# A recurrence and an MLP on one core: weight pieces dealt anew over the first four units, two turnings placed apart, and a little MLP work kept back

## The chip, the cores and the metric

The kernel runs on one core of one Trainium2 chip. The metric is device time in microseconds of one execution; the time of a kernel is the median of its runs. One further execution is profiled, and all views of the profile are of that one.

## What is computed

A gated linear recurrence over 768 steps for 4 batches and 8 heads of width 48, then an MLP over all 3072 tokens:

```python
f = 1.0 / (1.0 + np.exp(-f_logit))
for t in range(S):
    state = f[:, :, t, :, None] * state + np.einsum('bhd,bhe->bhde', k[:, :, t], v[:, :, t])
    y[:, :, t] = np.einsum('bhd,bhde->bhe', q[:, :, t], state)
x = y.transpose(0, 2, 1, 3).reshape(B * S, H * D)     # 3072 x 384
h = x @ w_in                                          # 384 x 2048
out = (h * (1.0 / (1.0 + np.exp(-1.702 * h)))) @ w_out
```

The MLP's arrays come as 64-bit floats. Their bits are read as pairs of 32-bit words, and the core makes 32-bit floats of them.

## The kernel before

**Units.** The tokens are cut into twelve units of 256 tokens (three for each batch). A unit's recurrence is done in chunks of 64: six levels of scores (`score`, L384), masked on VectorE (`evacuate`, L410), added into y (`add`, L448), with q and k multiplied by products of gates after each level (`promote`, L436 and L437, or L439 for both at once). `set_aside` (L423, ScalarE) keeps copies Kc and Qc of what the next level reads. `turn_k` (L505, L506) turns k through TensorE and copies it as kn. The states follow (products L523, chain on VectorE L538 to L543), then y takes what earlier states give (L563), is copied (L571) and brought to the MLP's layout xT by DMA (L592, L597). The first three units use a level at a time (parts "W"); from unit 3 on two levels go together (parts "V").

**Turnings.** Each unit's f, q and k arrive by rows and are turned: `begin_f` makes F = sigmoid(f), `begin` the q part of X, `begin_k` the k part. For units 0 to 2 TensorE turns them (L339, L342), from unit 3 on VectorE does (`nc.vector.transpose`, L327), and ScalarE adds the sigmoid of F (L332). After a turning SP's queue loads the same array for the unit after (`load_raw`), four DMAs each.

**Weights.** The 64-bit weights are 32 pieces, 128 columns of w_in or 128 rows of w_out each, fetched two at a time (`fetch_weights`, L180) into three buffers named bits. ScalarE makes a first copy `a` (L208), and five operations on VectorE make the piece (`chain`, L219 to L228). `convert` emits one such operation. When a pair is done, the next fetch is issued. A step of the MLP names how many pieces have to be done before it.

**MLP steps.** An h step is three matmuls with 256 columns (768 columns, L727), a sigmoid on ScalarE (sg, L732) and a product on VectorE (g, L733). An o step is one matmul of 384 columns (L755); each group of four is added into `sum` (L791, L793). From unit 3 on the second product runs as seven products of half size (L704), which need differences T of w_out, made on VectorE (`sums_of_b`, L622). PSUM's banks for h, o and the turnings are four, tag "mm".

**Order.** TensorE's order is the order of the program throughout. For the other engines it is so up to `fill_order.close()`, after unit 3; behind that a planner orders them. `merge(n, ...)` walks over the parts of unit n, and after each part emits MLP steps ("fill") up to a share of `columns`, and conversions up to a share of `pieces`. The shares come from `steady`: W 3, V 4, S 3, and 1 each for T, B and K. "Marks" below are the boundaries between merges: behind the first one the rest of unit 1 (its y and xT) comes at the head of unit 2, behind the second that of unit 2 at the head of unit 3. `hold=1` in merge 1 leaves its first part without fill. `UNIT` is 24576 columns, `LAG` 6912, `DM` 384.

For unit 2 the parts are W six times, B (f and q of unit 3), T, T, B (k of unit 3), S; for units from 3 on they are V three times, B (f and q), T, T, B (k), S.

Of the kernel before, what the change touches and what calls it, by code (L numbers as in the profile page):

```python
# [23 lines left out]
def kernel(  # L24
# [34 lines left out]
    B, H, S, D = q.shape  # L59
    DM = H * D  # L60
# [170 lines left out]
    def convert():  # L231

        if state["begin"] < len(pairs) and len(todo) <= NOP:
            begin_pair(state["begin"])
            state["begin"] += 1
        if todo and todo[0]:
            todo.pop(0)()
        if todo and todo[0] is None:
            todo.pop(0)
            state["done"] += 2  # L240
            fetch_weights()
# [34 lines left out]
    def load_vl(n, l):  # L276

        if n >= NALL:
            return
        t = vls[n, l] = ld.tile([P, DM], F32, tag=f"vl{l}", name=f"vl_{n}_{l}")  # L280
        if n < N_TURN:
            pt = ps.tile([P, DM], F32, tag="mm", name=f"tv_{n}_{l}", bufs=4)
            for g in range(NG):
                nc.tensor.matmul(
                    pt[g * 64:(g + 1) * 64], lhsT=perm[:, l - 1, :] if l else ident[:, ::2], rhs=vns[n][:, g, :],
                    start=True, stop=True,
                )
            nc.scalar.copy(t, pt)  # L288
            return
        nc.sync.dma_start(out=t, in_=v_toks[n % 2].rearrange("(n two m) e -> two n m e", two=2, m=LEV[l])[0])  # L290
# [507 lines left out]
    def mlp_blocks(*blocks):  # L798

        hs, os = zip(*(mlp_block(n, r) for n, r in blocks))  # L800
        return sum(hs, []) + sum(os, [])


    def keep_up(times):

        if times:
            pt = ps.tile([P, NL * 64], F32, tag="mm", name=f"idle_{next(serial)}", bufs=4)
        for _ in range(times):
            nc.tensor.matmul(pt, lhsT=ident, rhs=masks.rearrange("p l t -> p (l t)"), start=True, stop=True)

    units = [attention(n) for n in range(NALL)]
    LAG = 18 * DM

    def parts_of(n):

        parts = list(units[n][1])
        _, inter = parts.pop()
        if n:
            kind, scores = parts[0]
            _, ahead = units[n - 1][1][-1]  # L820
            parts[0] = kind, lambda: (ahead(), scores())
        if n < N_TURN:

            def with_v(l):
                kind, fn = parts[l]
                return kind, lambda: (fn(), load_vl(n, l) if n == 0 or l else None, keep_up(2 * (n == 0 and l < 3)))
            parts[:NL] = [with_v(l) for l in range(NL)]
        if n + 1 < NALL:
            begin_f, begin, begin_k, begin_gates = units[n + 1][0]
            i = len(parts)  # L830
            if n + 1 < N_FILL:

                parts.append(("K", lambda: (begin_k(), begin_gates(), load_vl(n + 1, 0) if n + 1 < N_TURN else None)))
                parts.insert(i - 4, ("B", begin if n == 0 else lambda: None))
                parts.insert(i - 5, ("B", begin_f))
                if n:

                    kind, head = parts[0]
                    parts[0] = kind, lambda: (head(), begin())
            else:  # L840
                kind, states = parts.pop()
                parts += [("B", begin_k), (kind, lambda: (states(), begin_gates()))]
                parts.insert(i - 3, ("B", lambda: (begin_f(), begin())))
        else:
            parts.append(("W", inter))
        return parts

    def merge(n, fill, columns, share, pieces=0, hold=0, by=1.0, chores=()):

        parts = parts_of(n)
        total = sum(share(kind) for kind, _ in parts)
        converting = {"W": 3, "T": 3, "B": 1} if n < N_FILL - 1 else {"W": 3, "V": 4, "S": 3, "T": 1, "B": 1}
        total_ops = sum(converting.get(kind, 0) for kind, _ in parts)
        held = sum(share(kind) for kind, _ in parts[:hold])
        at = at_ops = done = ops = 0
        for kind, fn in parts:
            ready = state["done"]
            fn()  # L860
            for chore in chores[:2]:
                chore()
            chores = chores[2:]
            at += share(kind)
            at_ops += converting.get(kind, 0)
            n_ops = min(int(pieces * NOP * at_ops / (by * total_ops)), pieces * NOP) - ops
            ops += n_ops
            first, n_columns = done, max(0, columns * (at - held) / (total - held) - done)

            def some(end):  # L870
                nonlocal done
                while fill and done < end and fill[0][2] <= ready:
                    w, emit, _ = fill.pop(0)
                    emit()
                    done += w
            for i in range(n_ops):
                some(first + n_columns * i / n_ops)
                convert()
            some(first + n_columns)
# [4 lines left out]
    UNIT = NFF * NK * U + U // P * NFF * DM  # L884
# [12 lines left out]
        load_raw(1, j)  # L897
    load_vn(1)
    fill = []
    merge(0, fill, 0, steady, 8)  # L900
    fill += mlp_blocks((0, 0)) + mlp_blocks((0, 1))
    merge(1, fill, UNIT // 2 - LAG // 2, steady, 10, hold=1)
    fill += mlp_blocks((1, 0), (1, 1)) + mlp_blocks((0, 2), (1, 2))
    merge(2, fill, UNIT, steady, 8)
    fill += mlp_blocks((2, 0), (2, 1)) + mlp_blocks((2, 2), (0, 3)) + mlp_blocks((1, 3), (2, 3))
    merge(3, fill, 3 * UNIT // 2 - LAG // 2, steady, 6, by=0.7)
    fill_order.close()
    for n in range(3, NALL):
        fill += mlp_unit(n)
# [33 lines left out]
```

## Time and profile before

| | us |
|---|---|
| median of 5 runs | 657.02 (655.54 to 658.23) |
| the profiled execution | 658.5 |
| its span, first to last instruction | 656.5 |
| TensorE busy (matmul; weight load) | 634.0; 543.2 |
| VectorE busy | 444.3 |
| ScalarE, GpSimd busy | 229.2; 60.1 |
| a turning on VectorE (L327) | 2.04 |
| the five operations of a piece | 0.35, 0.55, 0.35, 0.55, 0.54 to 0.59 |
| an h step, an o step on TensorE | 1.30, 0.65 |

The span is what lies between the first and the last instruction; the execution's own time has some 2 us around it. A matmul of 32-bit floats stands in the trace as two records, so an h step is six. The profile names engines PE (matmul), PEld (weight load), DVE (VectorE), ACT (ScalarE), POOL (GpSimd) and SP; a "q" behind the name is that engine's queue. "L327" is a line of the kernel. In lines of waits, "A <- B" says that A waited and B ended the wait.

### The profile page before, as it was taken

The page shows a single profiled execution, that of the slowest core. Times are in us where ns is not written, and L with a number is a line of the kernel's source. Part 1 is how long each engine was busy: PE and PEld are TensorE (multiplying, and loading weights), DVE is VectorE, ACT ScalarE, POOL GpSimd, SP SyncE. Part 2 cuts the span into 40 slices and gives each one's busy share as a digit, 9 for nine tenths or more (in the row PEclk, how much of TensorE's full clock was granted, in tenths as well). Part 3 has the DMA queues.
Part 4 walks back from the last instruction along what each step waited for, and adds up shares of the span by engine and source line. Part 5 has one row for each costly group of instructions (what it writes and reads, how often), then busy time and mean ns, then how long its engine had stood idle before and what let it go on. Part 6 is the DMA issues. An engine that isn't in the chain of part 4 may idle for free.

```text
span 656.5 us, 20397 instructions
## 1 busy us (share of the span) xinstructions
PE 634.0 (97%) x8958; PEld 543.2 (83%) x8958; DVE 444.3 (68%) x802; ACT 229.2 (35%) x477; POOL 60.1 (9%) x116
## 2 busy tenths in 40 slices
PE   6978989999999999999999999999999999999997
PEld 5655767766678689989989989989989989989997
DVE  2987977788887757657658658558558557553571
ACT  3454543243223423323324324324324334222120
POOL 3050020020001002002002002002002002000000
PEclk9998999999999999999999999999999999999999
DMA  8877875294125444524524524614604202101000
GB/s 185 223 198 186 210 180 130 81 225 82 37 64 148 136 105 111 151 50 119 148 44 121 150 43 120 163 29 120 166 27 104 67 25 62 39 2 26 25 1 24
DMA packets 67554, 67.67 MB, mean 103 GB/s; under 512 B 30410, under 2 KB 61290, under 8 KB 67466
## 3 DMA queue, kind: packets, MB, share of 16 engines
q1 hardware_dynamic: 67466, 66.38, 40.5%
q8 instruction: 70, 1.15, 0.8%
q14 instruction: 18, 0.15, 0.1%
HBM read 56.92 MB, written 8.65 MB: 100 GB/s over the span
## 4 chain that ended last, share of the span: by engine, by line
PE 86%; DVE 7%; DMA 3%; ACT 2%; issue 1%; SPq 1%; DVEq 0%; ACTq 0%
PE h L727 37%; PE o_X L704 7%; PE o L755 7%; PE o_Y L704 7%; PE o_Z L704 7%; PE sc L384 5%; PE y L448 5%; PE o_W L704 4%; PE t L339 2%; PE y L563 2%; PE sc L523 1%; DMA bits<-in_moe_w_in_dram 1%; PE tkn L505 1%; DMA xT<-yT 1%; DVE X L439 1%
## 5 line engine op out<-in xcount | busy, mean ns | idle before, releaser
L727 PE MATMUL h<-xT,w_in 128*128 128x256 f32 (+1 forms) x1152 | 261.4, 383 | 6.3 <-DMA xT<-yT 3.9
L727 PEld LDWEIGHTS h<-xT,w_in 128*128 128x128 f32 x1152 | 216.2, 191 | 40.1 <-issue 4.8
L733 DVE TENSOR_TENSOR g<-h,sg 128x256 f32<-128x256 f32 (+1 forms) x192 | 80.7, 422 | 99.9 <-ACT sg L732 97.4
L732 ACT ACTIVATE sg<-h 128x256 f32<-128x256 f32 (+1 forms) x192 | 73.3, 383 | 195.7 <-PE h L727 189.6
L423 ACT COPY Kc<-X 128x512 f32<-128x512 f32 x69 | 46.2, 670 | 118.7 <-DVE X L439 84.7
L755 PE MATMUL o<-w_out,g 128*128 128x384 f32 x192 | 66.1, 493 | 0.0
L439 DVE TENSOR_TENSOR X<-X,tot 128x1024 f32<-128x1024 f32 x45 | 55.1, 1224 | 15.4 <-PE sc L384 10.2
L755 PEld LDWEIGHTS o<-w_out,g 128*128 128x128 f32 x192 | 35.3, 190 | 22.9 <-issue 1.4
L704 PE MATMUL o_X<-w_out,g 128*128 128x192 f32 x288 | 51.9, 329 | 0.0
L704 PE MATMUL o_Y<-T,S 128*128 128x192 f32 x288 | 51.1, 331 | 0.1
L704 PEld LDWEIGHTS o_Y<-T,S 128*128 128x128 f32 x288 | 46.5, 190 | 2.6 <-DVE u L679 1.2
L704 PEld LDWEIGHTS o_X<-w_out,g 128*128 128x128 f32 x288 | 47.3, 190 | 0.9
L410 DVE TENSOR_TENSOR A<-sc,masks 128x512 f32<-128x512 f32 x72 | 46.7, 679 | 0.0
L376 POOL TENSOR_TENSOR tot<-F 128x512 f32<-128x512 f32 x12 | 12.5, 1040 | 342.6 <-DVE st L540 342.6
L448 PE MATMUL y<-A,vl 64*48 64x64 f32 x2304 | 40.9, 217 | 0.4 <-ACT vl L288 0.4
L448 PEld LDWEIGHTS y<-A,vl 64*48 64x48 f32 x2304 | 36.0, 120 | 3.8 <-issue 3.1
L327 DVE STREAM_TRANSPOSE X<-raw 128x1024 f32<-128x1024 f32 x18 | 36.7, 2039 | 2.5 <-PE y L563 2.5
L571 ACT COPY yT<-y 48x512 f32<-48x512 f32 x48 | 27.8, 580 | 14.0 <-PE y L563 13.5
L384 PEld LDWEIGHTS sc<-X,Kc 48*64 48x64 f32 x1344 | 23.9, 134 | 8.6 <-issue 3.8
L384 PE MATMUL sc<-X,Kc 48*64 48x64 f32 x1344 | 28.2, 220 | 1.8 <-DVE A L410 1.1
L376 POOL TENSOR_TENSOR tot<-tot 128x256 f32<-128x256 f32 (+4 forms) x60 | 27.3, 455 | 4.7
L357 POOL COPY q_last<-X 128x4 f32<-128x4 f32 x12 | 14.1, 1178 | 144.1 <-DVE X L327 111.8
(93 smaller groups left out, 675.4 us busy)
## 6 DMA issues: line engine op xcount, KB each, us to landing
vl<-v_tok SPq DMA_DIRECT2D x60, 192.0 KB, 2.9
bits<-in_moe_w_out_dram SPq DMA_DIRECT2D x8, 768.0 KB, 9.1
bits<-in_moe_w_in_dram SPq DMA_DIRECT2D x8, 576.0 KB, 9.0
v_tok<-in_v_dram SPq DMA_DIRECT2D x10, 384.0 KB, 4.4
vn<-v_tok SPq DMA_DIRECT2D x10, 384.0 KB, 7.1
xT<-yT SPq DMA_DIRECT2D x24, 144.0 KB, 2.8
raw<-in_q_dram SPq DMA_DIRECT2D x18, 192.0 KB, 4.0
raw<-in_f_logit_dram SPq DMA_DIRECT2D x18, 192.0 KB, 4.8
```

Of the source, the lines that this page charges most:

```text
L327: nc.vector.transpose(out.rearrange("p (a i j) -> p a j i", a=NP, j=R), raw[:, j].rearrange("p a (j d) -> p (a j) d", j=R)[:, :, :32],)
L376: nc.gpsimd.tensor_tensor(tn, t2[:, :, 0], t2[:, :, 1], ALU.mult)
L384: nc.tensor.matmul(out[g * HS:(g + 1) * HS, h, a, :], lhsT=lhs(h, a * U + g * G), rhs=rhs(h, a * U + g * G), start=True, stop=True,)
L410: nc.vector.tensor_tensor(A[:, :, c:c + w].rearrange("p h (x t) -> p h x t", t=64), t["sc"][:, :, c:c + w].rearrange("p h (x t) -> p h x t ...
L423: nc.scalar.copy(c.rearrange("p (n m) -> p n m", m=m), X[:, j, :NA].rearrange("p (n two m) -> p n two m", two=2, m=m)[:, :, hf, :],)
L439: nc.vector.tensor_tensor(qk, qk, by, ALU.mult)
L448: nc.tensor.matmul(dst(h, g, a), lhsT=vls[n, u][g * 64:(g + 1) * 64, (2 * a + h) * D:(2 * a + h + 1) * D], rhs=A(h, g, a), start=(start an ...
L704: nc.tensor.matmul(t[bank], lhsT=lhs(f), rhs=rhs(f), start=(new and f == 0), stop=(f == HF - 1), skip_group_check=True,)
L727: nc.tensor.matmul(ph, lhsT=w_in[:, c, ff * P:(ff + 1) * P], rhs=xTs[n][:, c, :], start=(c == 0), stop=(c == NK - 1))
L732: nc.scalar.activation(sg, ph, AF.Sigmoid, scale=1.702)
L733: nc.vector.tensor_tensor(g[ff // FG][:, ff % FG, :], ph, sg, ALU.mult)
L755: nc.tensor.matmul(t["po"], lhsT=g[ff // FG][:, ff % FG, tt * P:(tt + 1) * P], rhs=w_out[:, ff, :], start=(ff == ffs[0]), stop=(ff == ffs[ ...
```

## The change

Three edits. The first places the turning of q one part later than that of f, between the two T parts, for units from 3 on; this adds a part of share 1 to each of these units (25 shares become 26 in unit 2, 19 become 20 in later ones). The second deals the 32 pieces over the first four units as 6, 10, 9, 7 where it was 8, 10, 8, 6. The third takes 1152 columns of fill (3 x 384) out of merge 1 and puts them into merge 3; merge 2 has as many as before, so the kept steps pass through it.

```diff
             else:
                 kind, states = parts.pop()
                 parts += [("B", begin_k), (kind, lambda: (states(), begin_gates()))]
-                parts.insert(i - 3, ("B", lambda: (begin_f(), begin())))
+                parts.insert(i - 3, ("B", begin_f))
+                parts.insert(i - 1, ("B", begin))
...
-    merge(0, fill, 0, steady, 8)
+    merge(0, fill, 0, steady, 6)
     fill += mlp_blocks((0, 0)) + mlp_blocks((0, 1))
-    merge(1, fill, UNIT // 2 - LAG // 2, steady, 10, hold=1)
+    merge(1, fill, UNIT // 2 - LAG // 2 - 3 * DM, steady, 10, hold=1)
     fill += mlp_blocks((1, 0), (1, 1)) + mlp_blocks((0, 2), (1, 2))
-    merge(2, fill, UNIT, steady, 8)
+    merge(2, fill, UNIT, steady, 9)
     fill += mlp_blocks((2, 0), (2, 1)) + mlp_blocks((2, 2), (0, 3)) + mlp_blocks((1, 3), (2, 3))
-    merge(3, fill, 3 * UNIT // 2 - LAG // 2, steady, 6, by=0.7)
+    merge(3, fill, 3 * UNIT // 2 - LAG // 2 + 3 * DM, steady, 7, by=0.7)
     fill_order.close()
```

## The prediction, made before the changed kernel was run

> **What bounds the kernel now.** First I read the share of the span on the page (TensorE 97%), then cut the span into stages with the table of busy times by stretch. Its columns are the stretch, its length, then busy us and count for PE, PEld, DVE, ACT and POOL, then granted clock, DMA share and GB/s.
>
> ```profile
> 20.00:42.00 22.00, 18.35 (x478) 13.66 (x478) 22.00 (x50) 11.63 (x24) 5.08 (x1) 1.00 0.85 204
> 42.00:56.00 14.00, 9.66 (x216) 7.14 (x213) 8.89 (x21) 7.93 (x15) 5.07 (x10) 0.95 0.62 155
> 56.00:86.00 30.00, 30.00 (x505) 20.94 (x506) 28.43 (x68) 13.70 (x30) 0.00 (x0) 0.97 0.89 230
> 86.00:126.00 40.00, 38.30 (x533) 28.20 (x533) 29.71 (x64) 13.79 (x29) 3.63 (x6) 1.00 0.53 128
> 126.00:158.00 32.00, 28.38 (x318) 20.08 (x317) 27.61 (x47) 12.45 (x26) 3.75 (x8) 1.00 0.71 155
> 206.00:600.00 394.00, 393.92 (x5885) 356.73 (x5884) 256.49 (x414) 139.32 (x292) 35.55 (x62) 1.00 0.35 90
> ```
>
> From 206 to 600 us TensorE is idle for 0.08 us: nothing can be won there, only lost. All idle time that the change can reach lies before 158 us. Unit 0 (to 42 us) is VectorE's: 22.00 of 22. Unit 1 (56 to 86) is full on both, TensorE 30.00 and VectorE 28.43. After that TensorE bounds, with short gaps. Second view, TensorE's waits between 92 and 160 us (total, times, longest):
>
> ```profile
> PE h L727 <- DMA xT<-yT: 1.9, 2, 1.7
> PE h L727 <- ACT kn L506: 1.3, 1, 1.3
> PE y L563 <- DVE st L543: 0.7, 2, 0.5
> PE h L727 <- DVE sum L793: 0.5, 1, 0.5
> PE h L727 <- DVE g L733: 0.5, 1, 0.5
> ```
>
> The first is unit 1's first h step waiting for its xT; 1.7 of it lies at 95.8 us, behind the first mark. The second is at 131.8 us, and the timeline shows why: VectorE turns f and q back to back, F's sigmoid waits for the first, and the copy kn that frees a PSUM bank stands behind it on ScalarE.
>
> ```profile
> 127.79 2.04 DVE L327 STREAM_TRANSPOSE F<-raw 128x1024 f32<-128x1024 f32 x1
> 129.68 2.01 DVE L327 STREAM_TRANSPOSE X<-raw 128x1024 f32<-128x1024 f32 x1
> 34.51 0.99 ACT L208 ACTIVATE a<-bits 128x384 f32<-128x384 f32 x2 [2.04 <-DMA bits<-in_moe_w_out_dram]
> ```
>
> The last line is needed below: in unit 0 ScalarE stood 2.04 us for the fourth pair of weight pieces, which lands at 34.5 us.
>
> **What the Trainium skill says.** "Perfetto Trace Analysis", section Identifying the Most-Contended Engine, warns that TensorE's matmul share is no measure of how near it is to its peak, and offers the weight-load share. The trace agrees in direction: 97% matmul, 83% weight load. I therefore count idle time and not the share. The same page, section Optimizing Scalar/DVE Operations, says that an unsaturated VectorE that still causes bubbles elsewhere may be helped by breaking its work up; at 126 to 158 us it is 27.61 of 32 busy and makes the 1.3 us bubble, so that is the case of the split. "TensorE: Matmul & The Clock Gate", section What's actually happening, says that an idle window of about 3.4 us halves the clock. The trace has clock 0.95 and 0.97 in the second and third stretch, around the idle time before unit 0's first h steps: 12 records took 4.47 us there, against 2.59 later in the chain. That 1.9 us may come, go or move, and I put it into the range alone.
>
> **The deal of pieces, unit 0.** A piece costs VectorE five operations: from the groups of 14 to 42 us 0.351, 0.558, 0.345, 0.543 and 0.543 us, sum 2.34. Two pieces less are 4.68, and since neighbours overlap by about 0.08 each (start to start is shorter than the duration), ten operations are 4.68 - 0.8 = 3.9 us. One pair of ScalarE's a copies (1.0) goes too, and one fetch of 768 KB from SP's queue before unit 0 ends. VectorE is never idle there, so the 3.9 us lie on the path up to the state chain at 42.2 us. What is late next: the fourth pair's bits still land at 34.5, because SP issues them right behind unit 1's loads. Their a copies (1.0 us) now hold back the copies kn; from VectorE's side the last eleven operations end near 38.3, from ScalarE's side the second kn ends near 36.7, then 1.0 us of products. So the chain starts near 38.4, 3.8 earlier; I take **-3.6**, with 0 and -3.9 as the ends.
>
> **Unit 1.** It has ten pieces in both, at the same places, one pair later in the list. Its fill is taken until 8832 columns are reached, which whole steps make 9216 (eight h, eight o); with 7680 it is six h and eight o. So 1536 columns move, two h steps of 1.30 us (six records in the chain), 2.6 us of TensorE. VectorE sets the end: the third state product ends at about 86 us, just when TensorE arrives at y. Only one g (0.42) leaves the queue ahead of it, the other stood behind. So TensorE falls idle for 2.6 - 0.4 = 2.2 us at y: the removed fill shows as a gap. Behind the mark it comes back. Before, from y at 85.95 to h at 95.81 is 9.86 us, 1.9 of it waiting, thus about 7.9 of work. After, work is 7.9 + 2.6 = 10.5, longer than the path of xT (four copies, SP's issues, a landing), so the wait is gone. Net: -0.4 + (10.5 - 9.9) = **+0.2**; ends -1 and +1. By itself the shift of columns wins nothing here.
>
> **Unit 2.** Nine pieces for eight: five operations, 2.2 us, and two g more. From 86 to 126 us VectorE has 10.3 us free, so most of it is hidden beside fill. The end is not hidden: from F at 127.79 to the third state product at 143.2 VectorE is the chain (two turnings, four g, eight conversions, k's turning, 1.29 us for ScalarE's Kc and Qc, promote 1.23). After, F starts earlier: at 18/26 of the fill for 18/25, 681 columns or 1.15 us. F and q are apart, so F's sigmoid and kn follow while one turning (2.0) fits in the four PSUM banks (4 x 1.30 us), and the 1.3 us stall goes. But the chain has six g for four (+0.84). TensorE, free at T, waits at y for what VectorE still lacks. Net -1.15 + 0.84 = **-0.3**; ends +2.5 (all of the added work on the path) and -1.5. SP's four loads of the next q stand one part later, behind k's neighbours; they are needed a unit later.
>
> **Start of unit 3.** Before, eight o steps (5.2 us) lie ahead of unit 2's first h; after it is twelve, for 1536 columns are again kept. The waits 0.24 (xT), 0.55 (sum) and 0.51 (g, behind two T differences, 1.81 us together, on VectorE) come to 1.3. The T differences wait for a bits buffer that frees one pair later, behind the first g. I take **-1.0**; ends 0 and -1.3. Unit 3's five further operations meet VectorE at 80% and cost nothing while that cover holds; without it 2.2.
>
> **From unit 4 on** VectorE's order is the planner's, and the profile has F at 306.77 and q at 310.34, apart already: nothing, between -0.1 and the slower rival.
>
> **Sum**: -3.6 + 0.2 - 0.3 - 1.0 = -4.7 us. The profiled execution took 658.5 (span 656.5 and 2.0 around it), so 653.8 for one like it; it stands 1.5 above the median 657.0, which gives **652.3**.
>
> **The rivals.**
> Rival A, unit 0 hardly shrinks: the levels are a chain of promote 0.69, Kc 0.69, scores 0.7 and a weight landing, and the operations only fill its holes. For it: ScalarE's 2.04 us wait. Against: VectorE without any idle. Then unit 0 gives 0.5, unit 1 +0.2, the later steps half of theirs (-0.7): -1.0, **656.0**.
> Rival B, slower: q's turning, now placed nearer to k's, is put beside k by the planner in the seven turns of units 5 to 11. VectorE then has q 2.06, k 2.03, promote 1.22 and two sums 0.69 in a row, 6.7 us, while four banks of h last 5.2: 1.5 us of stall; the states, done at 305.9 for a y at 309.2, have 3.3 of slack for 4.1. I take 1.2 a unit, 8.4 in all: -4.7 + 8.4 = +3.7, **660.7**. It decides from 0.7 a unit (4.7 / 7). Against it: q can start as soon as y frees X, as at 310.34.
> That the split changes nothing after unit 3 is part of the forecast already.
>
> **The numbers.** About 0.3% (2 us) is what a measurement can tell here. Forecast 0.72, rival A 0.15, rival B 0.13; A falls within 0.3%, the forecast below it, B above. So faster 0.72, same 0.15, slower 0.13. The forecast's own range is 649.8 (-4.7, clock window gone -1.9, and the rest of unit 2) to 655; with A it reaches 657.3, and B stays out.
>
> **What would show it.** Right: unit 0's states start near 38.5 and its first h near 50; a new gap of about 2 us at y before unit 1's mark; no xT wait behind it; no wait on kn at unit 2's turnings; no sum and g waits at the start of unit 3; still no idle after 206 us. Wrong: states of unit 0 at 41 or later (A), or gaps that return once a unit after 250 us, with q next to k on VectorE (B).

## The result: no change, and the profile after

| | before | after |
|---|---|---|
| median of the runs made side by side | 657.9 us (79 runs, 654.8 to 662.8) | 658.1 us (44 runs, 655.7 to 664.6) |
| the profiled execution | 658.5 | 657.4 |
| its span | 656.5 | 655.3 |

The ratio of after to before is 1.0013, with a 95% interval of 1.0001 to 1.0026. A gain of 4.7 us (0.7%) was forecast, and none came.

First the table of busy times by stretch of the kernel after, with the stretches and columns of the prediction, and one more stretch, 158 to 192 us:

```profile
20.00:42.00 22.00, 21.28 (x560) 15.32 (x560) 21.26 (x48) 12.81 (x25) 1.32 (x3) 1.00 0.93 207
42.00:56.00 14.00, 11.75 (x266) 8.82 (x266) 11.75 (x25) 8.83 (x18) 3.88 (x8) 1.00 0.79 162
56.00:86.00 30.00, 28.13 (x483) 20.27 (x475) 27.00 (x64) 14.94 (x31) 3.46 (x6) 0.94 0.89 233
86.00:126.00 40.00, 39.48 (x455) 29.13 (x454) 30.96 (x66) 13.59 (x30) 0.00 (x0) 1.00 0.46 120
126.00:158.00 32.00, 28.66 (x434) 21.91 (x433) 28.02 (x51) 10.35 (x22) 3.95 (x8) 0.95 0.70 166
158.00:192.00 34.00, 30.61 (x240) 22.39 (x239) 27.52 (x51) 9.45 (x22) 0.02 (x1) 1.00 0.14 35
206.00:600.00 394.00, 394.00 (x5893) 358.13 (x5892) 256.49 (x415) 138.94 (x293) 34.75 (x62) 1.00 0.35 90
```

In unit 0 (first line) TensorE has become busier in the same 22 us, because it is further on. The steady part (last line) has no idle time, as before. New is the stretch from 158 us: TensorE is busy for 30.61 of 34.00 us. In the kernel before it had no idle time there:

```profile
158.00:192.00 34.00, 34.00 (x375) 25.76 (x375) 28.06 (x54) 9.03 (x22) 0.00 (x0) 1.00 0.09 25
```

Next, TensorE's waits of the kernel after from 20 to 206 us (total, times, longest):

```profile
PE y L563 <- DVE st L543: 3.3, 2, 2.9
PE sc L523 <- ACT kn L506: 2.3, 2, 1.9
PE h L727 <- DVE g L733: 2.0, 1, 2.0
PE o L755 <- DVE g L733: 1.4, 1, 1.4
PE h L727 <- DMA xT<-yT: 1.1, 1, 1.1
```

The waits that were to go are gone: the 1.7 us for xT behind the first mark, the 1.3 us for kn at unit 2's turnings, and those at the start of unit 3 (the xT wait left here is unit 0's). Two new ones for g stand in unit 3, of 2.0 us at 160 us and of 1.4 us at 187 us, and y of unit 2 now waits 2.9 us for its states. A table of milestones shows what that comes to. "y 1" is the first of the products L563 that close unit 1, at the first mark, "y 2" the same at the second mark, and so on; times are in us from the span's start, read in the timeline.

| | before | after |
|---|---|---|
| first product of y in unit 0 | 43.0 | 40.2 |
| first h step of unit 0 | 53.5 | 48.7 |
| y 1 | 85.9 | 80.8 |
| y 2 | 141.7 | 136.7 |
| from y 2 to y 3 | 70.2 | 74.0 |
| y 3 | 211.9 | 210.7 |

At y 2 the changed kernel is 5.0 us ahead with 2.6 us of MLP steps still owed (twelve h records fewer before y 1, 0.216 us each; by y 2 the debt stands as four o steps). Half of these are made up before y 3, so 1.3 us of the 74.0 are work. The other 2.5 us of the longer unit 3 are loss: TensorE stands idle for 3.9 us there where it stood 2.1 before, and its clock is halved for 3.4 us right behind y 2.

### The profile page after: what moved, and what is told of

Same layout as the page of the kernel before. It is cut to its first block, busy times and chain, and to the rows that moved or that the text cites. A ratio compares the mean times of both kernels' runs of the same rounds, so it can differ in the third digit from the quotient of the medians.

```text
span 655.3 us, 20390 instructions
## 1 busy us (share of the span) xinstructions
PE 633.5 (97%) x8958; PEld 544.4 (83%) x8958; DVE 444.3 (68%) x802; ACT 229.0 (35%) x477; POOL 54.0 (8%) x116
## 3 DMA queue, kind: packets, MB, share of 16 engines
q8 instruction: 70, 1.15, 0.8%
## 4 chain that ended last, share of the span: by engine, by line
PE 84%; DVE 7%; DMA 4%; ACT 2%; issue 1%; SPq 1%; ACTq 0%; DVEq 0%
PE h L727 35%; PE o_X L704 8%; PE o_Y L704 7%; PE o L755 7%; PE o_Z L704 7%; PE sc L384 5%; PE y L448 4%; PE o_W L704 4%; PE y L563 2%; DMA bits<-in_moe_w_in_dram 1%; PE sc L523 1%; PE tkn L505 1%; DMA bits<-in_moe_w_out_dram 1%; DMA vn<-in_v_dram 1%; PE t L339 1%
## 5 line engine op out<-in xcount | busy, mean ns | idle before, releaser
L704 PE MATMUL o_X<-w_out,g 128*128 128x192 f32 x288 | 53.7, 331 | 0.0
L704 PE MATMUL o_Z<-w_out,g 128*128 128x192 f32 x144 | 24.9, 326 | 0.0
```

Of the source, the lines that this page charges most:

```text
L704: nc.tensor.matmul(t[bank], lhsT=lhs(f), rhs=rhs(f), start=(new and f == 0), stop=(f == HF - 1), skip_group_check=True,)
```

## Experiments

All ratios are to the kernel before, run side by side on the same chip, with the 95% interval. "C" is the shift of 1152 columns, "D" the deal of pieces, "S" the split of the turnings. Theory A says that the split costs the change its gain in unit 2, at the 2.9 us gap before y 2; theory B says that it does so in unit 3 or behind.

### Each edit alone

C alone, against the kernel before:

```diff
-    merge(1, fill, UNIT // 2 - LAG // 2, steady, 10, hold=1)
+    merge(1, fill, UNIT // 2 - LAG // 2 - 3 * DM, steady, 10, hold=1)
...
-    merge(3, fill, 3 * UNIT // 2 - LAG // 2, steady, 6, by=0.7)
+    merge(3, fill, 3 * UNIT // 2 - LAG // 2 + 3 * DM, steady, 6, by=0.7)
```

> Only the third edit: 1152 columns (in whole steps 1536) out of merge 1 and into merge 3. Theory 1: VectorE sets the time of y at the end of units 1 and 2, so steps kept behind a mark leave TensorE idle ahead of it. Unit 1 pays about 2.2 us at y and gets back the 1.9 us wait for xT; unit 2 pays about 2.6 at y, because the same columns are passed on behind the second mark, and gets back some 1.3 at the start of unit 3. Sum about +1.5 us against the kernel before, idle before y in unit 2 near 3 us. The prediction's own reckoning (no loss at y in unit 2): about -0.8. A rival that blames the deal of pieces alone: 0.

Measured: **654.6 us, 0.9950 (0.9933 to 0.9966)**.

D alone, against the kernel before:

```diff
-    merge(0, fill, 0, steady, 8)
+    merge(0, fill, 0, steady, 6)
...
-    merge(2, fill, UNIT, steady, 8)
+    merge(2, fill, UNIT, steady, 9)
-    merge(3, fill, 3 * UNIT // 2 - LAG // 2, steady, 6, by=0.7)
+    merge(3, fill, 3 * UNIT // 2 - LAG // 2, steady, 7, by=0.7)
```

> Only the second edit: pieces 6, 10, 9, 7. Theory 1: unit 0's first h comes 4 to 5 us earlier and nothing of it is paid at y, as TensorE has its full fill; some is lost to weights that land late in unit 1. About -2.5 us against before. Theory 2 (VectorE's five added operations in unit 2 and five in unit 3 are the loss): the gain of unit 0 is given back at y in unit 2 and in unit 3, sum 0 or above.

Measured: **654.8 us, 0.9945 (0.9922 to 0.9968)**.

S alone, against the kernel before:

```diff
-                parts.insert(i - 3, ("B", lambda: (begin_f(), begin())))
+                parts.insert(i - 3, ("B", begin_f))
+                parts.insert(i - 1, ("B", begin))
```

> Only the first edit: q turned one part later than f. Both theories: the 1.3 us wait on kn at unit 2's turnings goes, but y in unit 2 is VectorE's, so it comes back there; between -0.7 and +0.3 us. A rival that blames the split (q's turning late, next to k's, holds g and the states back): +1 us or more, with TensorE idle at the turnings of units 2 and 3.

Measured: **657.9 us, 1.0009 (0.9991 to 1.0027)**. Two edits gain half a per cent each, and the third nothing. The shift of columns, to which the prediction gave nothing by itself, is one of the two that gain.

### Two of three

From here on the edits are shown against the changed kernel, unless another run is named. S and D, with the columns where they were:

```diff
-    merge(1, fill, UNIT // 2 - LAG // 2 - 3 * DM, steady, 10, hold=1)
+    merge(1, fill, UNIT // 2 - LAG // 2, steady, 10, hold=1)
...
-    merge(3, fill, 3 * UNIT // 2 - LAG // 2 + 3 * DM, steady, 7, by=0.7)
+    merge(3, fill, 3 * UNIT // 2 - LAG // 2, steady, 7, by=0.7)
```

> The changed kernel without its third edit (split and deal, columns as before). Each edit alone gave -3.3 (columns), -3.3 (deal) and about 0 (split), all three together about +0.2. Theory 1 (kept columns and early VectorE-set y clash: gaps at y in unit 2 and behind the T differences in unit 3): columns are the half of the clash that can be dropped, so this stays at the deal's own value, about -3.3 us against before. Theory 2 (the deal's added VectorE work in units 2 and 3 clashes with the split): about 0.

Measured: **654.8 us, 0.9962 (0.9945 to 0.9978)**.

D and C, without the split:

```diff
-                parts.insert(i - 3, ("B", begin_f))
-                parts.insert(i - 1, ("B", begin))
+                parts.insert(i - 3, ("B", lambda: (begin_f(), begin())))
```

> The changed kernel without its first edit (deal and columns together). Theory 1 (clash of deal and columns): about 0 against before, like the changed kernel. Theory 2 (clash of the split with the others): the two gains add or nearly so, -4 to -6 us against before.

Measured: **654.3 us, 0.9951 (0.9934 to 0.9968)**.

S and C, with the pieces dealt as before:

```diff
-    merge(0, fill, 0, steady, 6)
+    merge(0, fill, 0, steady, 8)
...
-    merge(2, fill, UNIT, steady, 9)
+    merge(2, fill, UNIT, steady, 8)
-    merge(3, fill, 3 * UNIT // 2 - LAG // 2 + 3 * DM, steady, 7, by=0.7)
+    merge(3, fill, 3 * UNIT // 2 - LAG // 2 + 3 * DM, steady, 6, by=0.7)
```

> The changed kernel without its second edit (split and columns). Theory 1: the columns' own gain stays, about -3 us against before. Theory 2: the split, earlier by a share in unit 2, with columns kept, leaves TensorE idle at y in unit 2, about -1 or less gain.

Measured: **657.8 us, 1.0008 (0.9991 to 1.0024)**. Beside the columns the split takes the whole gain back: C goes from 0.995 to 1.001 with it, C and D from 0.995 to 1.001. Without the columns it costs little or nothing (0.9945 to 0.9962 beside D, intervals overlapping). A second thing also shows: C and D do not add up. Together they gain 0.5%, as each does alone.

The loss beside C is not that of the changed kernel's two waits. From 140 to 206 us TensorE waits here for y 2 and hardly for g, and behind that wait the granted clock is halved for 6.8 us:

```profile
PE y L563 <- DVE st L543: 2.4, 2, 2.1
PE o L755 <- DVE g L733: 0.4, 1, 0.4
141.50:148.30 6.80, 6.47 (x132) 5.20 (x133) 6.63 (x14) 2.32 (x4) 3.38 (x6) 0.50 0.83 218
```

From y 2 to y 3 it took 72.0 us where C alone took 70.2, although TensorE was idle for less there (0.8 us against 1.5). So without the deal the gap at y 2, with the half clock behind it, may well be the cost, as the second theory above had it; no run tests that.

### Is it the gap at y 2?

The columns given back in merge 2 instead of merge 3, the rest as changed:

```diff
-    merge(2, fill, UNIT, steady, 9)
+    merge(2, fill, UNIT + 3 * DM, steady, 9)
...
-    merge(3, fill, 3 * UNIT // 2 - LAG // 2 + 3 * DM, steady, 7, by=0.7)
+    merge(3, fill, 3 * UNIT // 2 - LAG // 2, steady, 7, by=0.7)
```

> The changed kernel, but the 1152 columns are given back in merge 2 (UNIT + 3 * DM) in place of merge 3, so that behind the second mark about as much is left as before. Theory 1: the idle time before y in unit 2 falls from 3.3 us to about 1, the start of unit 3 waits some 0.5 to 1 more: about -2 us against the changed kernel, so about -1.8 against before. Theory 2 (VectorE's work in unit 2 sets the time whatever the fill): y in unit 2 moves later by as much, the sum is that of the changed kernel, about +0.2 against before.

Measured: **654.0 us, 0.9933 (0.9907 to 0.9959)**, the lowest ratio of all. But TensorE still stands before y 2, for 2.2 us, so the gain did not come from closing that gap. What is missing in this profile are the two waits for g in unit 3. TensorE's waits from 56 to 206 us:

```profile
PE y L563 <- DVE st L543: 3.1, 3, 2.2
PE h L727 <- ACT kn L506: 0.5, 1, 0.5
PE sc L384 <- DVE st L543: 0.4, 2, 0.2
PE sc L523 <- ACT kn L506: 0.2, 1, 0.2
```

Four idle matmuls of 384 columns put ahead of y 2, the rest as changed:

```diff
-            parts[0] = kind, lambda: (ahead(), scores())
+            parts[0] = kind, lambda: (keep_up(4 * (n == 3)), ahead(), scores())
```

> The changed kernel with four idle matmuls of 384 columns (2.6 us, results unused) on TensorE ahead of y at the head of unit 3's parts, where TensorE stands 2.9 us anyway. Theory 3 (the runs' clocks say so: about 3.1 windows of half clock an execution in the changed kernel and 1.6 before, each some 1 to 1.9 us): the gap no longer lowers the clock, about one window fewer, -1 to -2 us against the changed kernel. If gaps cost only their own length, the time stays that of the changed kernel, or is longer by up to 0.5.

Measured: **657.6 us, 1.0011 (0.9991 to 1.0031)**. The gap before y 2 and the half-clock stretch behind it are gone from the profile, and the time is what it was.

The split in unit 2 alone, and then from unit 3 on alone:

```diff
-                parts.insert(i - 3, ("B", begin_f))
-                parts.insert(i - 1, ("B", begin))
+                if n == 2:
+                    parts.insert(i - 3, ("B", begin_f))
+                    parts.insert(i - 1, ("B", begin))
+                else:
+                    parts.insert(i - 3, ("B", lambda: (begin_f(), begin())))
```

> The changed kernel, with f and q apart in unit 2 only. Theory A: as the changed kernel, between -0.5 and +0.8 us against before, a gap of 2 to 3 us at y in unit 2 and a half-clock window behind it. Theory B: about -3.

```diff
-                if n == 2:
+                if n > 2:
```

> The changed kernel, but f and q stay together in unit 2 and are apart only from unit 3 on. Theory A (the loss sits in unit 2 alone: between the two turnings VectorE stands in its order behind g steps whose sigmoid waits for ScalarE, so the states end later and TensorE has one long gap at y where it had two short ones): this is as good as the changed kernel without its split, about -3 us against before, and no half-clock window follows y in unit 2. Theory B (the split costs in units 3 and later): stays near +0.2.

Measured: **655.2 us, 0.9969 (0.9950 to 0.9988)** for unit 2 alone, although TensorE waits 2.9 us at y 2 there; **659.1 us, 1.0021 (0.9999 to 1.0044)** from unit 3 on. So theory A does not explain the loss of the whole change: the gap at y 2 is there in a kernel that keeps a gain, and the loss is there in a kernel without the gap. TensorE's waits of the second of these from 140 to 206 us are those of the changed kernel, with 0.6 us more at y 2:

```profile
PE h L727 <- DVE g L733: 1.9, 1, 1.9
PE o L755 <- DVE g L733: 1.4, 1, 1.4
PE y L563 <- issue: 0.6, 1, 0.6
```

### Unit 3 itself, or the planned units behind it?

Split in unit 3 alone, and then split everywhere but there, with the same condition:

```diff
-                if n == 2:
+                if n == 3:
```

> The changed kernel, but q's turning stands apart from f's only in unit 3; in unit 2 and from unit 4 on both are in one part again. Theory B (the split loses in unit 3 itself, through the two waits for g near 160 and 187 us): both waits are there, and the ratio to the kernel before is 1.000 or more. Rival (the loss comes from the units behind unit 3, where a planner orders the other engines): the ratio is 0.995, as without any split.

```diff
-                if n == 2:
+                if n != 3:
```

> The changed kernel with the split everywhere but in unit 3. Theory B: no wait of 2 us near 160 and none of 1.6 near 187 us, ratio 0.994 to 0.997. Rival (units behind unit 3): ratio 1.000 or more, with unit 3 free of both waits.

Measured: **657.9 us, 1.0011 (0.9992 to 1.0030)** in unit 3 alone; **654.1 us, 0.9953 (0.9932 to 0.9974)** everywhere but there. The first has both waits (2.4 and 1.4 us), the second has none in unit 3. So the loss that the split brings beside C and D is unit 3's.

### The place of the turning, or the share of the added part?

In the changed kernel TensorE's wait at 160 us ends 22 us before unit 3's first turning starts. A turning can't hold up what ran so much earlier; an added part can, since it thins the fill of the whole unit. So the part kept its place and lost its share, first in all units (`steady` gives 0 to the letter Q, and conversions take none from it either):

```diff
-                parts.insert(i - 1, ("B", begin))
+                parts.insert(i - 1, ("Q", begin))
```

> The changed kernel, all turnings of f and q apart, but the part that turns q has a share of 0: the fill and the conversions of each unit then stand as without the split, and only q's turning is placed later. If the shares do the harm (the wait near 160 us lies ahead of any turning of unit 3, so an added share can reach it and a moved turning can't): the wait of 2.1 us near 160 us goes, the one of 1.6 near 187 us may stay, and the ratio is 0.994 to 0.998. If the place of the turning does it: both waits stay, ratio 1.000 or more.

Measured: **654.5 us, 0.9982 (0.9962 to 1.0002)**. The wait at 160 is gone, and that at 187 too; one of 1.4 us at 163 stays, which the kernel without any split also has. The interval touches no change, so the same was done in unit 3 alone, and then, as a further edit to that, with the share put back for the conversions but not for the fill:

```diff
-                parts.insert(i - 1, ("B", begin))
+                parts.insert(i - 1, ("Q" if n == 3 else "B", begin))
```

> The whole change, with q's turning apart in every unit, but in unit 3 alone the added part has a share of 0 (fill and conversions there stand as without the split). If the share in unit 3 is the only loser: the two waits for g (2.1 us near 160, 1.6 near 187) go and the ratio is that of the split everywhere but in unit 3, 0.993 to 0.997. If the place of q's turning in unit 3 costs as well: 0.998 or more.

```diff
-        converting = {"W": 3, "T": 3, "B": 1} if n < N_FILL - 1 else {"W": 3, "V": 4, "S": 3, "T": 1, "B": 1}
+        converting = {"W": 3, "T": 3, "B": 1} if n < N_FILL - 1 else {"W": 3, "V": 4, "S": 3, "T": 1, "B": 1, "Q": 1}
```

> As the run with a share of 0 in unit 3, but the added part counts for the conversions again and only for the fill it has 0. If the fill's shift does the harm (one h step, 768 columns, less ahead of the part boundaries, so that its g falls behind the next part's work on VectorE): no waits, 0.993 to 0.997. If the shift of the conversions does it: both waits are back, 1.000 or more.

Measured: **655.8 us, 0.9974 (0.9954 to 0.9994)** and **655.9 us, 0.9967 (0.9944 to 0.9990)**. TensorE's waits of the first from 140 to 206 us are one line, and the second has none:

```profile
PE y L563 <- DVE st L543: 0.5, 1, 0.5
```

So in the changed kernel both waits need the fill's shift, and with one number changed in unit 3's shares the whole change gains 0.3%. That is less than the 0.5% of the split everywhere but in unit 3, and the intervals overlap, so a small cost of the turning's place is not ruled out. How a share does that is to be read in the timelines. The kernel after, from the second part's pair of promotions to the o step that waits (lines in between left out):

```profile
156.44 1.22 DVE L439 TENSOR_TENSOR X<-X,tot 128x1024 f32<-128x1024 f32 x1
158.95 1.23 DVE L439 TENSOR_TENSOR X<-X,tot 128x1024 f32<-128x1024 f32 x1 [1.29 <-ACT Qc L423]
160.10 1.28 DVE L410 TENSOR_TENSOR A<-sc,masks 128x512 f32<-128x512 f32 x2
161.76 0.42 DVE L733 TENSOR_TENSOR g<-h,sg 128x256 f32<-128x256 f32 x1
162.23 1.13 PE L727 MATMUL h<-xT,w_in 128*128 128x256 f32 x4 [1.98 <-DVE g L733]
...
184.53 2.04 DVE L327 STREAM_TRANSPOSE F<-raw 128x1024 f32<-128x1024 f32 x1
186.99 0.96 DVE L622 TENSOR_TENSOR T<-w_out,T 128x768 f32<-128x768 f32 x1
188.03 0.76 DVE L733 TENSOR_TENSOR g<-h,sg 128x256 f32<-128x256 f32 x2
188.51 1.88 PE L755 MATMUL o<-w_out,g 128*128 128x384 f32 x5 [1.41 <-DVE g L733]
```

The same two places in the kernel with a share of 0 in unit 3, in part:

```profile
158.58 0.42 DVE L733 TENSOR_TENSOR g<-h,sg 128x256 f32<-128x256 f32 x1
159.38 0.42 DVE L733 TENSOR_TENSOR g<-h,sg 128x256 f32<-128x256 f32 x1
159.72 0.95 DVE L622 TENSOR_TENSOR T<-w_out 128x768 f32<-128x768 f32 x1
160.58 1.22 DVE L439 TENSOR_TENSOR X<-X,tot 128x1024 f32<-128x1024 f32 x1
...
189.17 0.42 DVE L733 TENSOR_TENSOR g<-h,sg 128x256 f32<-128x256 f32 x1
189.51 2.03 DVE L327 STREAM_TRANSPOSE F<-raw 128x1024 f32<-128x1024 f32 x1
```

With the share at 0, the stretch of fill ahead of the second part's promotions has four g, and that ahead of F's turning seven. With the share at 1 it is three and five: one g falls behind two promotions, ScalarE's copy between them and a masking (from 156.44 to 161.76 us), and two fall behind F and a T difference (from 184.53 to 188.03). The arithmetic fits: merge 3 spreads 34560 columns. At the ends of the three V parts 4/20, 8/20 and 12/20 of them are 6912, 13824 and 20736, which whole steps meet exactly. With 4/19, 8/19 and 12/19 it is 364, 728 and 1091 columns more, and since an h step is 768 and steps are not cut, one h step more comes before the first boundary, two o steps before the second and two h steps before the third. VectorE's order up to `fill_order.close()` is the program's, so a g emitted after the boundary stands behind all of the next part.

The shift alone does not make a wait of 2 us, though. S and C without the deal have the same order, three g and five, and only 0.4 us of waiting: there the h steps of that stretch begin 0.7 us after the promotions (160.85 and 160.16 us), in the changed kernel 1.6 us before them (154.80 and 156.44). TensorE must also come early enough to run into the gap.

### Three more

Without the split and with the columns given back in merge 2:

```diff
-                parts.insert(i - 3, ("B", begin_f))
-                parts.insert(i - 1, ("B", begin))
+                parts.insert(i - 3, ("B", lambda: (begin_f(), begin())))
...
-    merge(2, fill, UNIT, steady, 9)
+    merge(2, fill, UNIT + 3 * DM, steady, 9)
...
-    merge(3, fill, 3 * UNIT // 2 - LAG // 2 + 3 * DM, steady, 7, by=0.7)
+    merge(3, fill, 3 * UNIT // 2 - LAG // 2, steady, 7, by=0.7)
```

> The changed kernel without its split and with the 1152 columns given back in merge 2. Without a split deal and columns together gave -3.2 against before; giving the columns back won 4 beside the split. If that win was the removal of waits at the start and end of unit 3 (2.2 and 1.6 us in the changed kernel), of which the kernel without split has only the second, 1.5, then about -4.5 us against before; if giving back only mends what the split broke, -3.2.

Measured: **656.1 us, 0.9971 (0.9952 to 0.9990)**, against 0.9951 with the columns given back in merge 3. Giving back in merge 2 helps with the split and not without it; the intervals overlap.

The order of the program kept over unit 4 too, so that T differences can run there:

```diff
-    fill_order.close()
...
     for n in range(4, NALL):
+        if n == 5:
+            fill_order.close()
```

> The changed kernel with the planner's freedom beginning one unit later, so that the T differences of w_out run in unit 4, not early in unit 3. Theory A': the waits in unit 3 (h on g 2.0, o on g 1.4) are VectorE's T differences ahead of g; they shrink to under 1 together and the time falls by 2 to 3 us against the changed kernel, about -2 against before, unless program order in unit 4 makes new gaps there. Rival: those waits come from the levels' own chain and the turning of f; the time stays at +0.2 or grows.

Measured: **661.6 us, 1.0058 (1.0035 to 1.0081)**. Only one of unit 3's waits is left in the profile, and a new one stands in unit 4. TensorE's waits from 206 to 300 us:

```profile
PE o_Y L704 <- DVE u L679: 2.2, 1, 2.2
PE h L727 <- DVE g L733: 0.4, 1, 0.4
```

So this run tells nothing about the T differences in unit 3; it shows only that keeping the program's order for a unit more costs time.

The split in unit 2 alone together with the columns given back in merge 2, against the run with the split in unit 2 alone:

```diff
-    merge(2, fill, UNIT, steady, 9)
+    merge(2, fill, UNIT + 3 * DM, steady, 9)
...
-    merge(3, fill, 3 * UNIT // 2 - LAG // 2 + 3 * DM, steady, 7, by=0.7)
+    merge(3, fill, 3 * UNIT // 2 - LAG // 2, steady, 7, by=0.7)
```

> Deal kept, split in unit 2 alone, and the 1152 columns given back in unit 2's merge instead of unit 3's. It joins the two forms that kept a gain. If their gains add: ratio 0.989 to 0.993 (about 3 to 5 us under the changed kernel and more). If unit 3 was the only loser, and giving back in unit 2 already avoided it: ratio 0.993, as giving back in unit 2 alone.

Measured: **653.7 us, 0.9952 (0.9922 to 0.9981)**. The gains do not add.

**The best version.** The lowest ratio, 0.9933, is the change with the columns given back in merge 2. Its interval overlaps with those of C alone, D alone, the two together, the split everywhere but in unit 3, and the run just above, among others. They all beat the kernel before; which of them is the fastest isn't settled.

## Why the prediction was wrong, point by point

**Unit 0, -3.6: right in mechanism, and near in size.** The state chain started at 39.0 us, where 38.5 was forecast; the first product of y came at 40.2 for 43.0 us, the first h step 4.8 us earlier. Fifteen other kernels here have the new deal and the same instructions up to there, and their first h steps lie between 48.1 and 54.0 us; the three latest (53.1 to 54.0) have the clock halved for 6.8 to 10.2 us ahead of that step. So one profile is a loose measure here. D alone gains 0.55%, or 3.6 us; that agrees with the step, though it is the sum of all that D does.

**Unit 1, +0.2: the claim that the removed fill shows as a 2.2 us gap was wrong.** The step said that VectorE sets the end of unit 1. From the first h step to y 1 the kernel before took 32.4 us, and the profiled run after 32.1, which looks like a confirmation. It isn't: TensorE has no such gap at y. It waited 1.9 us for kn, behind ScalarE's first copies of a weight pair that had not landed:

```profile
73.69 1.00 ACT L208 ACTIVATE a<-bits 128x384 f32<-128x384 f32 x2 [2.61 <-DMA bits<-in_moe_w_in_dram]
75.21 0.68 PE L523 MATMUL sc<-vn,kn 64*64 64x48 f32 x32 [1.87 <-ACT kn L506]
```

In the run with the columns given back in merge 2, whose program is the same up to there, the pair landed earlier:

```profile
72.05 1.02 ACT L208 ACTIVATE a<-bits 128x384 f32<-128x384 f32 x2 [0.86 <-DMA bits<-in_moe_w_in_dram]
```

and the stretch took 29.0 us; so it did in the splits in unit 2 alone, in unit 3 alone and everywhere but there (all 29.0). The 32.4 us of the kernel before, and of the deal alone, hold a half-clock stretch of 3.4 us each, and the profiled run of the kernel after has one too, behind the wait for kn. Split and deal with the columns as before, whose profile has no halved clock there, took 31.3 us. So taking 2.6 us of fill away shortens unit 1 by about 2.3 us, where the step allowed 0.4. The term that it had wrong is the price of y's wait: 2.2 us, where the profiles with 29.0 us show 0.7 us or less ahead of y and 0.5 behind its first products. Behind the mark the wait for xT went, as forecast (it was 1.7 us; the 1.9 of the step include 0.24 at the start of unit 3, which that step counts again). This may be why C alone gains 0.5% where the prediction gave it nothing, but its own profile does not show it: from the first h step to y 3 it took 157.7 us for 158.4 before, and 1.3 us of steps were still owed.

**Unit 2, -0.3: the sum came near by luck, by terms that were wrong.** F started 3.0 us earlier after y 1 (38.9 instead of 41.9), about the 1.15 of the step and the 1.7 of the xT wait. From F to the first state operation the prediction added only two g, 0.84 us. The kernel after took 16.1 us there for 13.1 before. Its timeline, in part:

```profile
119.67 2.04 DVE L327 STREAM_TRANSPOSE F<-raw 128x1024 f32<-128x1024 f32 x1
123.16 0.43 DVE L733 TENSOR_TENSOR g<-h,sg 128x256 f32<-128x256 f32 x1 [1.27 <-ACT sg L732]
124.80 0.42 DVE L733 TENSOR_TENSOR g<-h,sg 128x256 f32<-128x256 f32 x1 [0.76 <-ACT sg L732]
125.61 2.02 DVE L327 STREAM_TRANSPOSE X<-raw 128x1024 f32<-128x1024 f32 x1
129.94 2.01 DVE L327 STREAM_TRANSPOSE X<-raw 128x1024 f32<-128x1024 f32 x1
136.66 0.32 PE L563 MATMUL y<-X,st 48*48 48x64 f32 x4 [2.88 <-DVE st L543]
```

VectorE works in the order of the program, and between the two turnings now stand g operations for h steps that TensorE has not yet done; it waited 1.27 and 0.76 us for their sg. Before, f and q back to back let these pile up and then ran them off. The Trainium skill's "Perfetto Trace Analysis" (Optimizing Scalar/DVE Operations), on which the prediction leaned, says that breaking up instructions may let work be completed sooner. The split breaks up none, it sets two whole ones apart. Here the advice held for kn, whose 1.3 us wait went, and not for the end of the chain: the waits moved on to VectorE, and y 2 stood 2.9 us for its states. From y 1 to y 2 the time is 55.8 us before and after, with the same number of columns.

**Start of unit 3, -1.0, and unit 3's work at nothing: this is the step that failed.** With the step's -1.0 and the 1.3 us of columns that are made up here, the time from y 2 to y 3 should have been 70.2 - 1.0 + 1.3 = 70.5 us; it took 74.0. The waits at the start of unit 3 did go. But with the two new ones for g, of 2.0 and 1.4 us, TensorE's idle time rose from 2.1 to 3.9 us, where the step has it fall by 1.0; that is 2.8 of the 3.5 us. About 0.8 more is the half-clock stretch behind y 2: from the products of y to the first o step it is 3.55 us (137.44 to 140.99), and 2.75 before (142.50 to 145.25).

```profile
137.44 1.94 PE L563 MATMUL y<-X,st 48*48 48x64 f32 x60 [0.46 <-DVE st L543]
140.99 8.01 PE L755 MATMUL o<-w_out,g 128*128 128x384 f32 x24
142.50 1.45 PE L563 MATMUL y<-X,st 48*48 48x64 f32 x60 [0.47 <-DVE st L543]
145.25 5.43 PE L755 MATMUL o<-w_out,g 128*128 128x384 f32 x16
```

The first two lines are of the kernel after, the others of the kernel before. The working had the cause in its hands: for unit 2 it used the changed shares, 18/26 for 18/25 of the fill, and counted the earlier F as a gain. For unit 3 it wrote only that VectorE at 80% covers five more operations at no cost. It did not work out 20 shares for 19, nor what lands on the other side of a part boundary. It also had all idle time that the change can reach lie before 158 us, and both waits lie behind that. Mean load covers added work, but not a changed order on an engine that runs in order.

**From unit 4 on, 0: right.** No wait is listed from 206 to 600 us. Rival B, q's turning beside k's in every later unit, did not happen; the split everywhere but in unit 3 keeps the gain.

**Rival A** had unit 0 hardly shrink and named 656.0 us, a gain of 1.0. The measured +0.2 lies nearer to that than to the forecast, but by another way: unit 0 did shrink.

**What stays open.** Why the columns and the deal, 0.5% each, give 0.5% together and not 1.0. Without the split the pair has a wait of 1.4 us in unit 3 (o for g, at 163 us), which can be two fifths of what is missing. Why the split takes C's gain back without the deal is open too. With unit 3 mended, the change stands at 0.995 to 0.997, 2 to 3 us better than before and not 4.7. The granted clock may hold the rest, as the last section says.

## What to carry to other kernels

Where fill is dealt out by shares, a part added to one list moves every boundary in that unit, so work out for each boundary which steps slide over it and what then stands ahead of their consumers on an in-order engine. Taking filler away ahead of a mark can gain time even if it all has to be done later, as C alone did; that it does so where the filler delays the chain at that mark is likely here, but not shown. And test each edit of a combined change alone: here two of three gained half a per cent each, while the third, which showed no cost by itself, took it back.

## What the runs showed of the hardware

**Half a clock followed a gap when enough of it fell into one slot of 3.41 us.** In this stretch of the kernel after, right behind the wait at y 2, the column for the granted clock (the third from the right) reads 0.50:

```profile
137.50:140.90 3.40, 3.40 (x124) 3.40 (x124) 3.30 (x8) 1.42 (x3) 2.04 (x3) 0.50 0.82 155
```

In each of the twenty profiles the half-clock stretches begin a whole number of times 3.41 us apart; in the kernel after they begin at 14.61, 76.05 and 137.49 us, 61.4 us or eighteen times 3.41 from one to the next. So each run can be laid out in slots of that length. Between 12 and 300 us of all profiles, 24 slots at full clock hold 1.93 us or more of idle TensorE, and behind every one of them the clock was halved. Of 13 slots with 1.65 to 1.93 us, nine were followed by it; of some 1590 slots with less, two. So the length of a gap does not decide: the 2.0 us at 160 us fell into two slots, 1.1 and 0.9 us, and nothing followed, while the 1.9 us at 73 us fell into one, and the clock was halved from 76 us. The Trainium skill's "TensorE: Matmul & The Clock Gate" (What's actually happening) speaks of an idle window of about 3.4 us; here a slot idle for a little over half of that was enough. Why some stretches last 6.8 us instead of 3.4 stays open. Where the gap at y 2 was filled, the half-clock stretch was gone from there, and stood behind the next wait.

**How many there are differs from run to run, and the time goes with it.** From a run's mean granted clock and span one can work out how many such stretches of 3.4 us it had: (1 - clock) x span / 1.7, since each loses half of 3.4 us. The runs of the kernel before had 1.4 to 1.7 in the mean, those of the kernel after 3.1; C alone had 1.7, and 2.9 with the split beside it. A straight line through the 44 runs after gives 1.9 us for each, and 653.0 us with none; for the runs before it is 655.5 to 656.1 with none. By this estimate the change gains 2.5 to 3.1 us and pays about as much in clock; with the split in unit 2 alone, which has 3.0, the line ends at 649.5. It is a correlation: no run here set the number of stretches by itself, and filling one gap, with 2.6 us of idle matmuls, brought 1.9 stretches for 3.1 and no shorter time.
